# Weight scales, two loads and one block's last spectrum put earlier in a hand-written order of a four-layer S4 and SwiGLU kernel

## The chip, the cores and the metric

The kernel runs on one core of a Trainium2 chip. The metric is the device time of one execution in microseconds (us), the median of several runs. Lines are named by the line numbers of the kernel before (L776 is line 776); the engines are PE (TensorE, matmuls), DVE (VectorE), ACT (ScalarE), POOL (GpSimd) and SP (SyncE, which here only issues DMAs).

## The reference

Four layers work on 2048 tokens of width 512, in float32:

```python
x = A_u
x = x + _A_ref(_layernorm(x), ...)   # S4: K = Re(sum C exp(dt A l) dt B); FFT convolution over the tokens, + u * Dskip
x = x + _B_ref(_layernorm(x), ...)   # SwiGLU: (silu(x @ w_gate) * (x @ w_up)) @ w_down, inner width 1376
x = x + _A_ref(_layernorm(x), ...)   # the same K
x = x + _B_ref(_layernorm(x), ...)   # the same weights
```

The convolution's kernel K has 2048 lags for each of the 512 channels; it and the three FFN matrices are used by both pairs of layers.

## The kernel before, in words

**The work.** The tokens are cut into four blocks of 512. A unit of work is one (layer pair, block): layernorm, convolution, residual, layernorm, FFN, residual. The units run in the order (0,0), (0,1), (0,2), (1,0), (0,3), (1,1), (1,2), (1,3). The convolution is done with discrete Fourier transforms as matmuls: PE makes the spectrum of a block's normalised input (L296 for block 1, tile `pf`), ACT copies it out (L299, tile `u`) and SP stores it (L300, into `udr`); DVE multiplies spectra of inputs and of K (L776 `yk` or `t`, then sums and differences L781 and L782, tile `yf`); PE transforms back (L798, tile `pi`); DVE and ACT put pieces together (L748 to L757, L813 to L828). For each block this is done in eight **steps**, for two halves `h` of the channels and four groups `q` of frequencies, always in the order q = 0, 3, 1, 2. Block b also needs the products with the blocks ahead of it: their spectra are read back from DRAM by SP (L774, tile `uu`; the block's own by L716, tile `u`), and the spectra of K with them (L772, tile `w`).

**Stage one, up to about 257 us**, makes K in chunks of 64 channels. PE's last work in it are the `lags`, many small matmuls (L496, L497) into the PSUM tile `pk`; ACT copies that out (`spread_in`, L507). Its order is a plan, a list of functions with a time each (`at(t, ...)`). The plan also computes norms of the FFN weights (`weights`): squares on ACT (L333), column sums on PE (tile `nrm`, L336) and the largest of them on DVE (`largest`, L339), which empties a list `tops`. From these maxima `scales()` makes one scale for each weight matrix on DVE, in eleven small instructions (L344 to L356).

**The seam, about 257 to 345 us**, does the convolution of block 0, the last spectra of K, and makes f16 weights. Inside `tc.manual_schedule` the order of ACT, DVE, PE and POOL there is the order in which the code is written: `take(it, n)` runs n pieces of a generator. Its parts:

- `take(conv[h], 1)`: one of block 0's eight steps for half h (L776, L781, L782 on DVE, 8 matmuls L798 on PE). The inputs of both halves lie in the same four slots of a tile `mix`; the second half's quarters are loaded over the first's (L713 on SP) as these are used up.
- `first_parts` (PE L580, ACT L581, tile `w0r`) and `later_parts` (`odd`, `rest`: PE L531, ACT L598 or L599, DVE L600, SP store L538): spectra of K, for the block itself and for later blocks.
- `split(hi, lo, load)`: f16 weights in two pieces. ACT makes the high half (L664 for the gate and up matrices, L689 for the down matrix), DVE the low one (L669, L692), and `load` has SP load the next piece (L660, L683, L685), into `wsl` or a staging tile `st`. All three need the scales.
- `norm`: layernorm before the FFN of block 0: statistics on DVE (L203 to L209), ACT's `nn` (L843), PE's transposes (L845, tile `pt`), ACT L848. `direct_size()` (ACT L192, DVE L193) finds a maximum that later scales need.
- `second(*sec[-1])`: block 1's last spectrum (h=1, q=2), two pieces: 8 matmuls L296 from the saved normalised input `n`, then ACT L299 and SP L300.
- `block1`: the steps of block 1's convolution, `ssm(0, 1)`.

Behind the seam (from `product_scale()` on) a scheduler sets the order from priorities. SP's order in the seam is the scheduler's too: it is not one of the four engines of the manual order. Each DMA waits on SP until its tile's buffer is free, and what stands behind it waits as well. The tag `uu` has three buffers in turn: two hold block 1's normalised input for `second`, and the tiles `uu` of block 1's steps take the same ones afterwards.

Of the kernel before, what the change touches and what calls it, by code (L numbers as in the profile page):

```python
# [74 lines left out]
def kernel(ctx, tc, x, a_re, a_im, b_re, b_im, c_re, c_im, log_dt, d_skip,  # L75
# [12 lines left out]
    def tl(shape, name, tag, dt=F32):  # L88
        return sb.tile(shape, dt, name=name, tag=tag, bufs=BUFS[tag])

    def pbig(shape, name):
        return ps.tile(shape, F32, name=name, tag="big", bufs=2)
# [96 lines left out]
    def direct_size():  # L189

        da = tl([1, D], "da", "sg")
        A.activation(da, dsk, AF.Abs)  # L192
        V.tensor_reduce(dmax, da, axis=AX.X, op=OP.max)  # L193


    def stats(src, rows, scale, tag="stats", then=None):

        st = tl([P, 4, 6], "st", tag)
        mv = tl([P, 4, 2], "mv", tag)
        rs = tl([P, 8], "rs", tag)  # L200
        nb = rs[:, 4:]
        for r in range(rows):
            V.bn_stats(st[:, r], src[:, r])  # L203
            V.bn_aggr(mv[:, r], st[:, r])
        V.tensor_scalar(rs[:, :rows], mv[:, :rows, 1], EPS, 1.0 / scale ** 2, OP.add, OP.mult)
        G.tensor_tensor(rs[:, :rows], rs[:, :rows], mhalf[:, :rows], OP.pow)
        if then:
            then()
        V.scalar_tensor_tensor(nb[:, :rows], mv[:, :rows, 0], -1.0, rs[:, :rows], OP.mult, OP.mult)  # L209
        return rs, nb  # L210
# [79 lines left out]
    def direct(b, h, q, n, space=psml):  # L290

        pf = space([P, 2, HD], "pf")
        for i in range(2):
            for c in range(4):
                e = ek[q // 2][:, q % 2, c - 1, i] if c else ef[:, q, i]
                PE.matmul(pf[:, i], lhsT=e, rhs=n[c], start=c == 0, stop=c == 3)  # L296
        yield
        u = tl([P, NQ, 2, DC], "u", "uu")
        A.activation(parted(u), whole(pf), AF.Copy)  # L299
        nc.sync.dma_start(udr[0][b, h, q], u)  # L300
# [3 lines left out]
    def second(h, q, space=psml):  # L304
        if h not in halves:
            halves[h] = n = []
            for cp in range(2):
                t = tl([P, 2, HD], "n1", "uu")
                nc.sync.dma_start(t, ndr[h, cp])
                n += [t[:, 0], t[:, 1]]  # L310
        return direct(1, h, q, halves[h], space)
# [30 lines left out]
    def scales():  # L342
        c2 = sb.tile([P, 3], F32, name="c2")
        V.tensor_reduce(c2, cmx, axis=AX.X, op=OP.max)  # L344
        V.tensor_scalar(c2, c2, 1.01, None, OP.mult)
        ex = sb.tile([P, 3], I32, name="ex")
        V.tensor_scalar(ex, c2.bitcast(I32), 23, None, OP.logical_shift_right)
        V.tensor_scalar(ex, ex, 67, -125, OP.max, OP.add)
        V.tensor_scalar(ex, ex, 1, None, OP.arith_shift_right)
        bits = sb.tile([P, 6], I32, name="bits")  # L350
        V.tensor_scalar(bits[:, 0:3], ex, -1, 141, OP.mult, OP.add)
        V.tensor_scalar(bits[:, 3:4], ex[:, 0:1], 1, 105, OP.mult, OP.add)
        V.tensor_scalar(bits[:, 4:5], ex[:, 0:1], -1, 111, OP.mult, OP.add)
        V.tensor_tensor(bits[:, 5:6], ex[:, 0:1], ex[:, 1:2], OP.add)
        V.scalar_tensor_tensor(bits[:, 5:6], bits[:, 5:6], 107, ex[:, 2:3], OP.add, OP.add)
        V.tensor_scalar(sc6.bitcast(I32), bits, 23, None, OP.logical_shift_left)  # L356
# [143 lines left out]
    def skip(ch, kt, eng):  # L500

        k = kt[0:1, :, 0]
        eng.tensor_tensor(k, k, dsk[:, ch * DC:(ch + 1) * DC].rearrange("p (g d) -> p g d", g=4), OP.add)

    def spread_in(pk):
        ks = tl([P, 4, 16, 16], "ks", "nn")
        A.activation(ks, pk.rearrange("p d (c a) -> p a c d", a=4), AF.Copy)  # L507
        return ks
# [120 lines left out]
    def take(it, n):  # L629
        for _ in range(n):  # L630
            next(it, None)
# [200 lines left out]
    def first_norm(nn2):  # L832


        rows = TB // P
        xt = xs[0][:, :rows]
        nh, nlo = nhl2[:, 0, 0], nhl2[:, 0, 1]
        rs, nb = stats(xt, rows, 256.0, "stats2", then=lambda: split(0, 1))
        yield
        pt = pbig([P, rows, 4, P], "pt")  # L840
        for r in range(rows):
            nn = nn2[:, r]
            A.activation(nn, xt[:, r], AF.Identity, scale=rs[:, r:r + 1], bias=nb[:, r:r + 1])  # L843
            for k in range(4):
                PE.transpose(pt[:, r, k], nn[:, k * P:(k + 1) * P], ident)  # L845
        ptv = pt.rearrange("p r k t -> p k r t")
        nhv = nh.rearrange("p k (r t) -> p k r t", r=rows)
        A.activation(nhv, ptv, AF.Copy)  # L848
        yield
        V.tensor_tensor(nlo.rearrange("p k (r t) -> p k r t", r=rows), ptv, nhv, OP.subtract)  # L850
        yield
# [89 lines left out]
    prods, tops = [], []  # L941
# [11 lines left out]
    with tc.manual_schedule(engines={mybir.EngineType.Activation, mybir.EngineType.DVE, mybir.EngineType.PE, mybir.EngineType.Pool}):  # L953
# [53 lines left out]
        sec = [(h, q) for h in range(2) for q in QORD]  # L1007
        plan = []

        def at(t, f, n=1):  # L1010
            plan.append((t, len(plan), (lambda: take(f, n)) if hasattr(f, "__next__") else f))
# [20 lines left out]
        def factors(c, t):  # L1032

            at(t + 0.2, lambda: upper(ts[c]))

            def tiles(c):
                gs[c] = tl([P, 2, 32, DC], "g", ("ga", "gb")[c % 2])
            if c == 1:
                at(t + 0.1, lambda: tiles(c))
            if c + 1 < NCH:  # L1040
                at(t + 8.05, lambda: tiles(c + 1))
            gg, ge = later(lambda: gen_g(c, ts[c], gs[c])), later(lambda: gen_e(ts[c]))
            for k in range(4):
                at(t + 0.2 + 2 * k, gg, 2)
            at(t + 0.3, ge)
            for k in range(5):
                at(t + 8.2 + k, gg)
            for k in range(4):
                at(t + 22.0 + 0.6 * k, ge, 1 if k < 3 else 100)
# [27 lines left out]
        def weights(n, t0, t1, t2, t3):  # L1077

            us = []

            def product():
                for s, p, m in us:
                    p()
                    if m:
                        tops.append(m)

            def largest():
                while tops:
                    tops.pop(0)()
            at(t0, lambda: us.extend(u for u in (next(nrm, None) for _ in range(n)) if u))  # L1090
            at(t1, lambda: [u[0]() for u in us])
            at(t2, product)
            at(t3, largest)

        starts = [0.0, 31.0, 62.0] + [93.0 + 28.0 * k for k in range(NCH)]
        for i in range(NCH - 1):
            t = starts[i]
            use(i, t)
            factors(i + 1, t)
            second_block(i, t)  # L1100
            if i + 2 < NCH:
                prepare(i + 2, t)
            for k, t0, t1, t2, t3 in ((0, -13.0, 0.25, 13.9, 22.3), (1, 0.3, 14.5, 17.45, 22.9),
                                      (2, 15.0, 26.5, 28.05, 36.0)):
                n = ((3, 3, 0), (3, 3, 0), (3, 3, 0), (3, 2, 0), (3, 2, 0), (3, 3, 0), (3, 3, 3))[i][k]
                if i == NCH - 2 and k == 2:
                    t0, t1, t2, t3 = 15.0, 20.0, 24.0, 27.0
                if n:
                    weights(n, t + t0, t + t1, t + t2, t + t3)
        t = starts[NCH - 1]  # L1110
        late = starts[NCH - 2] + 12.0
        plan.sort()
# [23 lines left out]
        def split(hi, lo, load=0):  # L1136
            for _ in range(load):
                loads.pop(0)()
            for _ in range(hi):
                his.pop(0)()  # L1140
            for _ in range(lo):
                los.pop(0)()
# [13 lines left out]
            yield from itertools.cycle([w[:, j] for w in (wz, wm) for j in range(2)])  # L1156
        slots = slots()

        ks = spread_in(pk)
        odd = later_parts(c - 1, kts[0], (3, 1))  # L1160
        rest = later_parts(c, kts[1])
        bb1 = tl([P, 2, 2, 2, HD], "bb1", "n")
        norm = first_norm(tl([P, 2, D], "nn1", "hf"))
        take(conv[0], 1)
        spread_pe(ks, kts[1])
        skip(c, kts[1], G)
        take(conv[0], 1)
        scales()
        split(1, 0)
        first_parts(c, 0)  # L1170
        take(conv[0], 1)
        split(1, 1)
        split(0, 0, 1)
        first_parts(c - 1, 3)
        split(1, 0)
        take(conv[0], 1)
# [13 lines left out]
        split(0, 0, 1)  # L1190
        take(odd, 2)
        take(conv[1], 1)
        direct_size()
        block1 = ssm(0, 1)
        take(norm, 1)
        take(rest, 2)
        take(odd, 1)
        take(norm, 1)
        take(block1, 1)
        take(rest, 1)  # L1200
        take(odd, 2)
        split(1, 0)
        take(odd, 1)
        take(norm, 1)
# [9 lines left out]
        split(0, 0, 3)  # L1214
        sizes(c, kts[1], ks)
        nn2 = tl([P, 2, D], "nn2", "nn")
        take(second(*sec[-1]), 2)
    pscale = product_scale()
    with tc.high_priority(offset=BOOST // 2):
        while los:  # L1220
# [50 lines left out]
```

## Time and profile before

| what | value |
|---|---|
| runs of the kernel before | median 1156.48 us (1155.17 to 1157.27, 3 runs) |
| the profiled execution's own time | 1156.48 us |
| its span, first to last instruction | 1154.7 us |
| PE busy | 1100.2 us (95%) |
| DVE busy | 998.7 us (86%) |
| ACT busy | 599.1 us (52%) |
| POOL busy | 109.5 us (9%) |

The span is what the views of the trace cover; the 1.8 us around it belong to the execution's own time. Three views are used. The **timeline** lists one engine's instructions: start in us from the span's start, duration in us, engine, line, operation, output<-inputs with shapes, count, and in brackets how long the engine stood idle just before and what ended that idle time. The **waits** add those brackets up by instruction and releaser: us in total, times, longest. The **windows** give for a stretch each engine's busy time with the number of instructions, then the granted PE clock (1 is full speed), the DMA engines' busy share and GB/s. A **DMA issue** row gives the size and the us from the issue's start to the landing of its data.

### The profile page before, as it was taken

To read this page: it belongs to the slowest core of one execution; us is meant where nothing else is said; L and a number is where in the kernel's file an instruction comes from. 1 tells how busy PE (TensorE), PEld (TensorE's weight loads), DVE (VectorE), ACT (ScalarE), POOL (GpSimd) and SP (SyncE) were. 2 spreads that over 40 slices of the span, in tenths; PEclk is the share of its full clock that TensorE was granted. 3 is DMA by queue.
4 is the path that set the end of the run, shared out by engine and by line. 5 is a ranking of instruction groups with operands and counts; after the bars stand their busy time and mean duration, and the time that the engine had idled before them with its cause. 6 is when DMAs were issued, how large, how long until landed. Compare 5 with 4: busy or idle time off the path is not lost.

```text
span 1154.7 us, 24400 instructions
## 1 busy us (share of the span) xinstructions
PE 1100.2 (95%) x9942; PEld 877.6 (76%) x9942; DVE 998.7 (86%) x1585; ACT 599.1 (52%) x1198; POOL 109.5 (9%) x163
## 2 busy tenths in 40 slices
PE   2989999998889999999999999999999999999998
PEld 1878888887776868686868687877778686876875
DVE  8999999988889899999899999989994999973211
ACT  6989889734553453567453534555434352334211
POOL 0112222210000010011010001111000100000000
PEclk9989999999899999999999999999999999999999
DMA  5367777867473446332253454343444145312000
GB/s 209 128 165 165 161 185 170 193 186 244 164 240 110 129 139 207 111 102 74 89 153 124 133 156 150 107 120 105 147 121 140 50 130 160 97 37 48 14 24 19
DMA packets 127314, 150.38 MB, mean 130 GB/s; under 512 B 50897, under 2 KB 75985, under 8 KB 127202
## 3 DMA queue, kind: packets, MB, share of 16 engines
q1 hardware_dynamic: 115298, 123.32, 34.9%
q0 software_dynamic: 11904, 25.50, 9.5%
q8 instruction: 78, 1.28, 0.5%
q14 instruction: 34, 0.28, 0.1%
HBM read 98.70 MB, written 33.82 MB: 115 GB/s over the span
## 4 chain that ended last, share of the span: by engine, by line
PE 35%; DVE 23%; issue 8%; DMA 5%; ACT 3%; SPq 1%; POOL 1%; DVEq 0%; ACTq 0%; POOLq 0%
PE pgu L911 6%; PE pgu L912 6%; PE pgu L914 6%; PE py L926 4%; PE py L927 3%; PE py L928 3%; DVE t L776 3%; DVE yk L779 3%; PE pi L798 2%; PE pf L280 2%; DMA w<-wdr 2%; DVE yk L776 2%; DVE z L228 2%; DVE sg L918 1%; DMA mix<-nn 1%
## 5 line engine op out<-in xcount | busy, mean ns | idle before, releaser
L911 PE MATMUL pgu<-mix,wsl 128*128 128x256 f16 x1280 | 299.0, 273 | 4.3 <-DVE sg L918 3.3
L912 PE MATMUL pgu<-mix,wsl 128*128 128x256 f16 x1280 | 298.6, 273 | 0.0
L914 PE MATMUL pgu<-mix,wsl 128*128 128x256 f16 x1280 | 195.7, 273 | 0.0
L912 PEld LDWEIGHTS <-wsl 128*128 128x128 f16 x1280 | 125.4, 98 | 21.2 <-issue 4.8
L926 PE MATMUL py<-wsl,hh 128*128 128x512 f16 (+1 forms) x352 | 133.4, 379 | 6.1 <-DVE xg L931 4.5
L911 PEld LDWEIGHTS <-wsl 128*128 128x128 f16 x1280 | 125.3, 98 | 16.1
L914 PEld LDWEIGHTS <-wsl 128*128 128x128 f16 x1280 | 125.4, 98 | 14.8
L928 PE MATMUL py<-wsl,hl 128*128 128x512 f16 (+1 forms) x352 | 133.4, 379 | 0.8 <-DVE hl L920 0.8
L776 DVE TENSOR_TENSOR t<-uu,w 128x1024 f32<-128x1024 f32 x96 | 116.9, 1217 | 6.6 <-DMA w<-wdr 6.4
L917 ACT ACTIVATE sg<-pgu,sc 128x512 f32<-128x512 f32 x80 | 54.6, 682 | 130.0 <-PE pgu L914 126.8
L927 PE MATMUL py<-wsl,hh 128*128 128x512 f16 x320 | 121.3, 379 | 0.0
L779 DVE TENSOR_TENSOR yk<-yk,t 128x1024 f32<-128x1024 f32 x96 | 116.8, 1216 | 0.2
L918 DVE SCALAR_TENSOR_TENSOR sg<-pgu,sc,sg 128x512 f32<-128x512 f32 x80 | 59.6, 745 | 52.0 <-ACT sg L917 51.8
L531 PE MATMUL pw<-kt,ek 128*128 128x256 f32 (+1 forms) x384 | 91.8, 376 | 0.0
L919 ACT ACTIVATE hh<-sg 128x512 f16<-128x512 f32 x80 | 50.1, 627 | 76.3 <-DVE sg L918 76.3
L531 PEld LDWEIGHTS pw<-kt,ek 128*128 128x128 f32 x384 | 73.3, 195 | 8.6
L798 PE MATMUL pi<-yl,mix 128*128 128x256 f16 x576 | 78.9, 272 | 0.6 <-DVE yl L228 0.3
L280 PE MATMUL pf<-z,eh 128*128 128x256 f16 x576 | 74.9, 273 | 0.8 <-DVE z L228 0.6
L776 DVE TENSOR_TENSOR yk<-u,w0r 128x1024 f32<-128x1024 f32 x56 | 68.2, 1217 | 0.8 <-ACT u L282 0.8
L920 DVE TENSOR_TENSOR hl<-sg,hh 128x512 f16<-128x512 f32 x80 | 54.8, 685 | 15.5 <-ACT hh L919 15.5
L496 PE MATMUL pk<-re,g 128*32 128x64 f32 x1024 | 65.1, 317 | 2.4 <-DMA g<-g 2.4
L927 PEld LDWEIGHTS <-hh 128*128 128x128 f16 (+1 forms) x352 | 34.5, 98 | 42.7 <-issue 7.3
(238 smaller groups left out, 2164.3 us busy)
## 6 DMA issues: line engine op xcount, KB each, us to landing
uu<-udr SPq DMA_DIRECT2D x96, 256.0 KB, 3.0
w<-wdr SPq DMA_DIRECT2D x96, 256.0 KB, 2.7
udr<-u POOLq DMA_DIRECT2D x32, 256.0 KB, 2.6
g<-g POOLq DMA_DIRECT2D x6, 1024.0 KB, 9.0
udr<-u SPq DMA_DIRECT2D x16, 256.0 KB, 3.5
n<-xdr SPq DMA_DIRECT2D x4, 1024.0 KB, 5.6
kdr<-ks SPq DMA_DIRECT2D x6, 512.0 KB, 2.9
kt<-kdr SPq DMA_DIRECT2D x24, 128.0 KB, 3.1
```

What stands on the lines that cost most here:

```text
L280: PE.matmul(pf[:, o], lhsT=e, rhs=m, start=k == 0, stop=k == len(terms) - 1)
L531: PE.matmul(pw[:, i], lhsT=e, rhs=kt[:, :, c + 4 * k0:4 * k1:4, :].rearrange("p g k d -> p k g d"), start=c == 0, stop=c == 3)
L776: V.tensor_tensor(t, uu.unsqueeze(2).to_broadcast([P, NQ, 2, 2, DC]), w.unsqueeze(3).to_broadcast([P, NQ, 2, 2, DC]), OP.mult)
L779: V.tensor_tensor(yk, yk, t, OP.add)
L798: PE.matmul(pi[:, o], lhsT=e, rhs=m, start=k == 0, stop=k == len(terms) - 1)
L911: PE.matmul(o, lhsT=wgu(wi, k, 0)[:, fs], rhs=nh[:, k], start=k == 0, stop=False)
L912: PE.matmul(o, lhsT=wgu(wi, k, 1)[:, fs], rhs=nh[:, k], start=False, stop=False)
L914: PE.matmul(o, lhsT=wgu(wi, k, 0)[:, fs], rhs=nlo[:, k], start=False, stop=k == 3)
L918: V.scalar_tensor_tensor(sg, pgu[:, 1], sc6[:, 4:5], sg, OP.mult, OP.mult)
L926: PE.matmul(py[:, r], lhsT=hh[:n, f, rc], rhs=wd(f, 0)[:n], start=f == 0, stop=False)
L927: PE.matmul(py[:, r], lhsT=hh[:n, f, rc], rhs=wd(f, 1)[:n], start=False, stop=False)
L928: PE.matmul(py[:, r], lhsT=hl[:n, f, rc], rhs=wd(f, 0)[:n], start=False, stop=f == FT - 1)
```

## The change

Nothing is computed otherwise; instructions stand at other places.

1. The plan's last `weights` group leaves out its `largest`; the code behind the last lags empties `tops` itself, then runs `scales()` and `split(1, 0)` (ACT's first high half, of a gate piece), all ahead of `spread_in` (ACT's copy L507 of the lags). Before, `scales()` and that half stood behind block 0's second step.
2. That piece's low half (`split(0, 1)`) and the load of the next one (`split(0, 0, 1)`) stand ahead of block 0's second step instead of behind its third.
3. `direct_size()` stands behind the first piece of `norm`.
4. The generator of block 1's last spectrum is made ahead of `norm`; its matmuls and two of `odd`'s parts stand ahead of the norm's transposes, its copy and store right behind them. Before, it was the last thing of the seam, and the two parts stood behind block 1's first step.

```diff
--- before.py
+++ after.py
@@ -1090,7 +1090,8 @@
             at(t0, lambda: us.extend(u for u in (next(nrm, None) for _ in range(n)) if u))
             at(t1, lambda: [u[0]() for u in us])
             at(t2, product)
-            at(t3, largest)
+            if t3:
+                at(t3, largest)
 
         starts = [0.0, 31.0, 62.0] + [93.0 + 28.0 * k for k in range(NCH)]
         for i in range(NCH - 1):
@@ -1104,9 +1105,9 @@
                                       (2, 15.0, 26.5, 28.05, 36.0)):
                 n = ((3, 3, 0), (3, 3, 0), (3, 3, 0), (3, 2, 0), (3, 2, 0), (3, 3, 0), (3, 3, 3))[i][k]
                 if i == NCH - 2 and k == 2:
-                    t0, t1, t2, t3 = 15.0, 20.0, 24.0, 27.0
+                    t0, t1, t2, t3 = 15.0, 20.0, 24.0, None
                 if n:
-                    weights(n, t + t0, t + t1, t + t2, t + t3)
+                    weights(n, t + t0, t + t1, t + t2, t3 and t + t3)
         t = starts[NCH - 1]
         late = starts[NCH - 2] + 12.0
         plan.sort()
@@ -1156,21 +1157,25 @@
             yield from itertools.cycle([w[:, j] for w in (wz, wm) for j in range(2)])
         slots = slots()
 
+        while tops:
+            tops.pop(0)()
+        scales()
+        split(1, 0)
         ks = spread_in(pk)
         odd = later_parts(c - 1, kts[0], (3, 1))
         rest = later_parts(c, kts[1])
         bb1 = tl([P, 2, 2, 2, HD], "bb1", "n")
+        last = second(*sec[-1])
         norm = first_norm(tl([P, 2, D], "nn1", "hf"))
         take(conv[0], 1)
         spread_pe(ks, kts[1])
         skip(c, kts[1], G)
+        split(0, 1)
+        split(0, 0, 1)
         take(conv[0], 1)
-        scales()
-        split(1, 0)
         first_parts(c, 0)
         take(conv[0], 1)
-        split(1, 1)
-        split(0, 0, 1)
+        split(1, 0)
         first_parts(c - 1, 3)
         split(1, 0)
         take(conv[0], 1)
@@ -1190,15 +1195,17 @@
         split(0, 0, 1)
         take(odd, 2)
         take(conv[1], 1)
-        direct_size()
         block1 = ssm(0, 1)
         take(norm, 1)
+        direct_size()
         take(rest, 2)
         take(odd, 1)
+        take(last, 1)
+        take(odd, 2)
         take(norm, 1)
+        take(last, 1)
         take(block1, 1)
         take(rest, 1)
-        take(odd, 2)
         split(1, 0)
         take(odd, 1)
         take(norm, 1)
@@ -1214,7 +1221,6 @@
         split(0, 0, 3)
         sizes(c, kts[1], ks)
         nn2 = tl([P, 2, D], "nn2", "nn")
-        take(second(*sec[-1]), 2)
     pscale = product_scale()
     with tc.high_priority(offset=BOOST // 2):
         while los:
```

On DVE, at the end of stage one, the rows of the kernel before read (`cmx` the maxima, `wo` spectra of K, `sc_92` the scales, of whose eleven instructions the first and last are shown, `st_2533` the staged gate piece):

```order
L339 TENSOR_REDUCE cmx<-nrm 128x1
L563 TENSOR_TENSOR wo<-pw,wo 128x2x6x64
L776 TENSOR_TENSOR yk<-mix,w0r 128x1024
...
L776 TENSOR_TENSOR yk<-mix,w0r 128x1024
...
L344 TENSOR_REDUCE c_2718<-cmx 128x3
...
L356 TENSOR_SCALAR sc_92<-bits 128x6
L776 TENSOR_TENSOR yk<-mix,w0r 128x1024
...
L669 SCALAR_TENSOR_TENSOR wsl_2665<-st_2533,sc_92,wsl_2665 128x2x344
L669 SCALAR_TENSOR_TENSOR wsl_2666<-st_2533,sc_92,wsl_2665 128x2x344
```

and those of the changed kernel

```order
L563 TENSOR_TENSOR wo<-pw,wo 128x2x6x64
L339 TENSOR_REDUCE cmx<-nrm 128x1
L344 TENSOR_REDUCE c_2673<-cmx 128x3
...
L356 TENSOR_SCALAR sc_92<-bits 128x6
L776 TENSOR_TENSOR yk<-mix,w0r 128x1024
...
L669 SCALAR_TENSOR_TENSOR wsl_2664<-st_2532,sc_92,wsl_2664 128x2x344
L669 SCALAR_TENSOR_TENSOR wsl_2665<-st_2532,sc_92,wsl_2664 128x2x344
L776 TENSOR_TENSOR yk<-mix,w0r 128x1024
```

The scales moved ahead of block 0's first step, and the two low halves from behind the third step to behind the first. On ACT the high half that they wait for now stands ahead of the copy L507.

On SP, around the same time, the rows of the kernel before read (`mix<-udr` are the reloads of block 0's inputs for the second half, `xg` the residual input, `wsl` and `st` weights):

```order
L713 DMA mix<-udr_114 128x512 x2
L232 DMA xg<-in_A_u_dram 128x4x512
L660 DMA wsl_2668<-in_B_w_up_dram 128x4x344
L660 DMA wsl_2668<-in_B_w_gate_dram 128x4x344
L660 DMA wsl_2668<-in_B_w_up_dram 128x4x344
L232 DMA xg<-in_A_u_dram 128x4x512
L713 DMA mix<-udr_114 128x512
L660 DMA st_2758<-in_B_w_gate_dram 128x4x344
L713 DMA mix<-udr_114 128x512
```

and those of the changed kernel

```order
L713 DMA mix<-udr_114 128x512
L232 DMA xg<-in_A_u_dram 128x4x512
L660 DMA wsl_2667<-in_B_w_up_dram 128x4x344
L660 DMA wsl_2667<-in_B_w_gate_dram 128x4x344
L660 DMA wsl_2667<-in_B_w_up_dram 128x4x344
L660 DMA st_2725<-in_B_w_gate_dram 128x4x344
L232 DMA xg<-in_A_u_dram 128x4x512
L713 DMA mix<-udr_114 128x512 x3
```

The second reload stood ahead of all six large loads and now stands behind them. The staged piece's load moved ahead of the second `xg`.

Further on in SP's rows, where block 1 begins, the kernel before has one load `uu` far earlier, between the staging load and the first of the stores L538 ahead of the reloads, and then here

```order
L685 DMA st_3046<-in_B_w_down_dram 96x512
L538 DMA wdr<-wos 128x3x128
L716 DMA u<-udr_114 128x512
L772 DMA w<-wdr 128x512
L538 DMA wdr<-wos 128x3x128
L716 DMA u<-udr_114 128x512
```

and the changed kernel

```order
L685 DMA st_3058<-in_B_w_down_dram 96x512
L538 DMA wdr<-wos 128x3x128
L716 DMA u<-udr_114 128x512
L774 DMA uu<-udr_114 128x512 x2
L300 DMA udr_114<-u 128x512
L774 DMA uu<-udr_114 128x512 x2
L772 DMA w<-wdr 128x512
```

The first load `uu` of block 1's steps moved here from far ahead, behind a load `u`, and with it come three more loads and the last spectrum's store. On PE, at the transposes, the kernel before has four parts L531 (16 matmuls `pw`) behind block 0's last step, then the transposes `pt`; the changed kernel has

```order
L531 MATMUL pw<-kt_429,ek_83 128x192 x3
L296 MATMUL pf<-n_1626,ef 128x256
L296 MATMUL pf<-n_1626,ek_84 128x256
L296 MATMUL pf<-n_1628,ek_84 128x256 x2
L296 MATMUL pf<-n_1626,ef 128x256
L296 MATMUL pf<-n_1626,ek_84 128x256
L296 MATMUL pf<-n_1628,ek_84 128x256 x2
L531 MATMUL pw<-kt_429,ef 128x192
L531 MATMUL pw<-kt_429,ek_83 128x192 x3
L531 MATMUL pw<-kt_429,ef 128x192
L531 MATMUL pw<-kt_429,ek_83 128x192 x3
L845 MATMUL pt<-ident,nn_2691 128x128 x8
```

Sixteen matmuls, the last spectrum's eight and two parts, moved from behind the transposes to ahead of them.

## The prediction

> **What bounds the kernel now.** I read the totals first, then the windows over the seam and behind it, then the waits, and the timelines last. All sums are made against the profiled execution: 1156.48 us, of which the span is 1154.7 and 1.8 lie around it. It is also the median of the runs shown, so no correction is needed. A measurement of this kernel can tell about 0.2%, 2.3 us, from no change.
>
> The first line is the page's totals. The others are windows: width, busy time (instructions) of PE, its weight loads, DVE, ACT and POOL, then granted clock, DMA share, GB/s.
>
> ```profile
> PE 1100.2 (95%) x9942; PEld 877.6 (76%) x9942; DVE 998.7 (86%) x1585; ACT 599.1 (52%) x1198; POOL 109.5 (9%) x163
> ```
>
> ```profile
> 260.00:270.00 10.00, 10.00 (x79) 8.82 (x68) 6.49 (x10) 6.16 (x7) 0.31 (x1) 1.00 1.06 385
> 290.00:300.00 10.00, 5.21 (x22) 4.92 (x21) 9.83 (x18) 4.18 (x8) 1.34 (x1) 0.66 0.41 142
> 350.00:400.00 50.00, 48.57 (x376) 36.66 (x375) 45.41 (x90) 20.07 (x43) 2.42 (x4) 1.00 0.39 126
> 400.00:450.00 50.00, 48.27 (x405) 36.58 (x403) 49.90 (x80) 26.11 (x49) 6.22 (x7) 1.00 0.49 144
> 350.00:1154.00 804.00, 790.37 (x6585) 607.13 (x6583) 673.55 (x1123) 347.27 (x672) 53.79 (x67) 1.00 0.36 107
> ```
>
> The whole is bound by PE: behind the seam it is busy 790.4 of 804 us. Inside the seam it is not: at 290 to 300 DVE is at 9.8 of 10, and PE falls to 5.2. There DVE sets the pace, and so it does at 400 to 450, where it is at 49.9 of 50. The one place with room on DVE is 350 to 400, 4.6 us. What the change saves on PE counts only as far as DVE lets PE keep it.
>
> The waits of the seam (us in total, times, longest):
>
> ```profile
> ACT ks L507 <- PE pk L497: 7.3, 1, 7.3
> DVE wsl L669 <- ACT wsl L664: 4.8, 1, 4.8
> PE pt L845 <- ACT nn L843: 4.8, 1, 4.8
> DVE t L776 <- DMA w<-wdr: 3.7, 2, 2.6
> PE pgu L911 <- DVE sg L918: 3.3, 1, 3.3
> PE pi L798 <- DVE yf L781: 2.9, 2, 2.7
> DVE wsl L692 <- ACT wsl L689: 2.0, 2, 1.8
> DVE mix L600 <- ACT mix L599: 1.1, 1, 1.1
> ```
>
> The change aims at the second, third and fifth of these.
>
> **Part 1 and 2, scales, first high half and low half.** DVE's and ACT's timelines:
>
> ```profile
> 249.96 0.96 DVE L563 TENSOR_TENSOR wo<-pw,wo 128x768 f32<-128x768 f32 x1 [0.66 <-ACT w0r L559]
> 248.78 0.52 DVE L339 TENSOR_REDUCE cmx<-nrm 128x1 f32<-128x344 f32 x1 [2.08 <-PE nrm L336]
> 250.83 1.22 DVE L776 TENSOR_TENSOR yk<-mix,w0r 128x1024 f32<-128x1024 f32 x1
> 252.88 1.26 DVE L776 TENSOR_TENSOR yk<-mix,w0r 128x1024 f32<-128x1024 f32 x1
> 254.86 0.15 DVE L344 TENSOR_REDUCE c<-cmx 128x3 f32<-128x6 f32 x1
> 256.52 1.23 DVE L776 TENSOR_TENSOR yk<-mix,w0r 128x1024 f32<-128x1024 f32 x1
> 263.34 1.78 DVE L669 SCALAR_TENSOR_TENSOR wsl<-st,sc,wsl 128x688 f16<-128x688 f32 x2 [4.79 <-ACT wsl L664]
> 265.04 1.22 DVE L776 TENSOR_TENSOR yk<-mix,w0r 128x1024 f32<-128x1024 f32 x1
> 268.36 1.22 DVE L776 TENSOR_TENSOR yk<-mix,w0r 128x1024 f32<-128x1024 f32 x1
> 270.46 1.23 DVE L776 TENSOR_TENSOR yk<-mix,w0r 128x1024 f32<-128x1024 f32 x1
> ```
>
> ```profile
> 264.58 0.28 ACT L581 ACTIVATE w0r<-pw 128x128 f32<-128x128 f32 x1 [1.27 <-PE pw L580]
> 268.19 0.37 ACT L581 ACTIVATE w0r<-pw 128x256 f32<-128x256 f32 x1
> ```
>
> The eleven scale instructions take 1.66 us (254.86 to 256.52) wherever they stand. With L563 done at 250.9 and the maximum 0.52 behind it, the scales are ready at about 253.0 instead of 256.5. ACT then makes the first high half in the 7.3 us in which it waited for the lags, and the DVE wait of 4.79 goes. From 253.0 a step costs 2.05 (250.83 to 252.88) and the low half 1.7 to 1.8: the fourth step starts at 253.0 + 3 × 2.05 + 1.78 = 260.9. The fourth to the fifth took 3.32, so the fifth could start at 264.3; but its `w0r` comes from ACT at 264.86, behind a PE that is busy 10.00 of 10.00 there. It starts at 264.9 instead of 268.36. The sixth's `w0r` comes at 268.56, so by these rows alone it starts at 268.6 instead of 270.46: **-1.9 us**. More of the 4.79 isn't to be had, since PE is late next.
>
> **What the moved loads cost.** The sixth step reads the second reload L713, which now stands on SP behind both `xg` and four weight loads. SP's timeline, and the DMA issues of three stretches: the second `xg`, the reload issued right behind it, and the two reloads ahead of all large loads (size, us from issue to landing):
>
> ```profile
> 257.18 0.38 SPq L232 DMA_DIRECT2D xg<-in_A_u_dram  x1
> 259.60 1.73 SPq L232 DMA_DIRECT2D xg<-in_A_u_dram  x1
> ```
>
> ```profile
> xg<-in_A_u_dram SPq DMA_DIRECT2D x1, 1024.0 KB, 11.4
> mix<-udr SPq DMA_DIRECT2D x1, 256.0 KB, 10.3
> ...
> mix<-udr SPq DMA_DIRECT2D x2, 256.0 KB, 3.1
> ```
>
> The loads cannot start before 257.2, when the lags free their buffers. The second `xg` was issued at 259.60 and landed 11.4 later, 271.0. By the window's 385 GB/s, one of 688 KB takes 1.85 us and one of 256 KB takes 0.7. With the staged piece now ahead of `xg` and the reload behind, the reload lands at 271.0 + 1.85 + 0.7 = 273.5. The sixth step then starts 3.1 later than before, not 1.9 earlier: **+3.1 us** on DVE. The bounds are -1.9 (the reload overtakes) and +3.1. I take +3.1, since the reload issued behind the large loads needed 10.3 us for the same 256 KB that took 3.1 ahead of them.
>
> The Trainium skill, "DMA: Bandwidth & Descriptors", section "Queues, rings and completion order", says that each DMA engine consumes a ring in order but that completion is not FIFO per issuing engine. If the second half let the reload finish first, the term would be -1.9. The 11.4 us row of the second `xg`, which fits a queue emptied in order, speaks against it here.
>
> PE's gap ahead of the seventh transform, 2.7 us in the waits, grows by the same lateness to about 5.2.
>
> **Part 3, `direct_size`.** Its DVE maximum leaves the chain ahead of the norm's last factor L209: **-0.6 us**.
>
> ```profile
> 290.19 0.67 DVE L193 TENSOR_REDUCE dmax<-da 1x1 f32<-1x512 f32 x1
> 294.28 0.15 DVE L209 SCALAR_TENSOR_TENSOR rs<-mv,rs 128x2 f32<-128x2 f32 x1
> 294.81 1.21 DVE L776 TENSOR_TENSOR yk<-u,w0r 128x1024 f32<-128x1024 f32 x1
> 295.95 1.22 DVE L776 TENSOR_TENSOR t<-uu,w 128x1024 f32<-128x1024 f32 x1
> ```
>
> L209 then stands at 294.28 + 3.1 - 0.6 = 296.8.
>
> **Part 4, the last spectrum.** On PE it fills the wait for the norm. Windows of PE alone (width, PE busy, clock, DMA share, GB/s):
>
> ```profile
> 279.60:283.20 3.60, 3.60 (x8) 0.54 0.12 12
> 295.30:299.70 4.40, 4.37 (x17) 0.50 0.87 294
> 328.00:330.60 2.60, 2.54 (x13) 0.50 0.80 109
> ```
>
> The idle 4.79 and the half clock behind it (4.4 us at 0.50, so 2.2 lost) go: -7.0 on PE. The wait of 3.3 ahead of `pgu` and its half clock (2.6 at 0.50, 1.3 lost) should go too, since ACT no longer makes so many high halves ahead of the first activation of the FFN: -4.6. Against these stand +2.5 ahead of the seventh transform and, since DVE is late, a new wait at the third `pgu` for the second L918, about 3.5 and 1.7 of half clock. PE's own sum is -7.0 - 4.6 + 2.5 + 5.2 = **-3.9 us**.
>
> The Trainium skill, "TensorE: Matmul & The Clock Gate", section "What's actually happening", has the clock halve after an idle window of about 3.4 us. Here 2.73 us idle were enough (0.54 at 279.6 to 283.2). By the page the gap ahead of the seventh transform would start to cost clock only now, 1.8 us more; by the rows it costs that already, and I count none.
>
> On DVE the same move costs a wait. Block 1's first load `uu` had a free buffer and was issued long ahead, before the reloads; now the last spectrum's tiles hold it longer, and on SP it stands behind the load `u`, which waits until DVE has done `yk`.
>
> ```profile
> 296.06 0.34 SPq L716 DMA_DIRECT2D u<-udr  x1
> ```
>
> ```profile
> uu<-udr SPq DMA_DIRECT2D x96, 256.0 KB, 3.0
> ```
>
> L716 was issued at the end of `yk` (294.81 + 1.21). Now `yk` ends near 298.6, `uu` is issued by 299.5 and lands 3.0 later, at 302.5; DVE, in order, could have used it at 298.5. That is **+4.1 us**. The bounds are 0, if other DVE work moved ahead covers it, and 4.7, with slower landings as near the large loads; I take the row's median.
>
> **The sum.** DVE: +3.1 - 0.6 + 4.1 = 6.6. The waits of 1.1 (L600) and 1.8 (L692) go, because DVE now comes later than ACT: 3.7. Of the 3.7 us for `w` in block 1's next steps I count half as gone, 1.9, because SP issues some of those loads earlier and some later: 1.8. A wait for the FFN's activation L917 takes their place, 1.2: **+3.0 us** at the end of the seam. PE is 3.9 ahead by its own sum, but its transforms for block 1 wait for DVE, and DVE is then full to 450 but for the 4.6 us at 350 to 400. I count none of these as absorbed, since DVE waits there for products of PE and ACT that come as late. Forecast: 1156.5 + 3.0 = **1159.5**, its own range 1157.8 to 1162.
>
> **The rivals.**
>
> 1. *The reload isn't held* (it overtakes, or lands with the small loads). Then the term +3.1 is -1.9: 3.0 - 5.0 = -2.0, with a little of the first wait following, about 1154. For it speaks that the loads run on 16 engines; against it the landing rows. The page of the Trainium skill named above, "DMA: Bandwidth & Descriptors", would allow it; no row here shows it. Chance 0.15.
> 2. *PE sets the end.* DVE's lag is taken up by its 4.6 us at 350 to 400, and PE keeps its -3.9: 1152.6. For it speaks PE's 98% behind the seam; against it DVE's 49.9 of 50. Chance 0.15.
> 3. *The uu wait is short.* Where the last spectrum's store and loads go early, the +4.1 is about 1: 3.0 - 3.1 = -0.1, 1156.4. Chance 0.16.
> 4. *Nothing is given back.* Stalls add: +3.1 - 0.6 + 4.7 + 1.2 = 8.4, less the 1.1 and 1.8 that must go, is 5.5, with one more half-clock stretch of up to 1.7: 1162 to 1164. For it speaks that each PE wait was followed by half clock. Chance 0.17.
>
> Rivals 1 and 2 end on the other side: rival 2 decides when DVE's idle at 350 to 400 falls by more than 3 us.
>
> **How the numbers follow.** The forecast has 0.37; some three quarters of it (0.27) lie over 1158.8, so slower is 0.27 + 0.17 = 0.44, same 0.10 + 0.16 = 0.26, faster 0.15 + 0.15 = 0.30. The range 1152.5 to 1164 reaches from rival 2 to rival 4.
>
> **What would show it.** Right: no wait at the first L669; the sixth step waits for `mix` and starts near 273.5; PE idle of 5 us ahead of the seventh transform, none ahead of `pt`; DVE waits some 4 us for `uu` near 300. Wrong: the sixth step at 268.6; `uu` landed before DVE asks; DVE's idle at 350 to 400 near 1.5.

## The result, and the profile after

The changed kernel takes 1160.6 us (median) against 1156.03 for the kernel before in the same series: 1.0037 times as long, interval 1.0026 to 1.0048. It is slower by 4.6 us where 3.0 were forecast. One of its six executions took 1620.7 us at a granted clock of 0.66 and is left out of the ratio; the other five lie between 1159.1 and 1161.5. Its profiled execution took 1160.61 us with a span of 1158.8, so 1.8 us lie around the span as before, and the two profiles differ by 4.1.

The waits of PE and DVE in the seam of the changed kernel, the larger rows (us in total, times, longest):

```profile
DVE yk L776 <- DMA mix<-udr: 7.8, 1, 7.8
PE pi L798 <- DVE yf L781: 6.8, 2, 5.3
...
DVE t L776 <- DMA udr<-u: 5.5, 1, 5.5
PE pgu L911 <- DVE sg L918: 5.4, 1, 5.4
...
PE pw L531 <- DVE wos L600: 1.7, 1, 1.7
DVE wsl L692 <- ACT wsl L689: 1.4, 1, 1.4
DVE sg L918 <- ACT sg L917: 1.2, 1, 1.2
```

The waits that the change aimed at are gone: no row for L669 behind ACT's L664, none for the transposes `pt`. Two DVE waits on transfers stand in their place, 7.8 and 5.5 us. DVE's timeline at the two places, and at the norm's last factor (L209) between them:

```profile
264.54 1.22 DVE L776 TENSOR_TENSOR yk<-mix,w0r 128x1024 f32<-128x1024 f32 x1 [0.56 <-ACT w0r L581]
274.41 1.23 DVE L776 TENSOR_TENSOR yk<-mix,w0r 128x1024 f32<-128x1024 f32 x1 [7.84 <-DMA mix<-udr]
...
297.66 0.15 DVE L209 SCALAR_TENSOR_TENSOR rs<-mv,rs 128x2 f32<-128x2 f32 x1
297.73 0.67 DVE L193 TENSOR_REDUCE dmax<-da 1x1 f32<-1x512 f32 x1
...
298.79 1.20 DVE L776 TENSOR_TENSOR yk<-u,w0r 128x1024 f32<-128x1024 f32 x1
305.51 1.23 DVE L776 TENSOR_TENSOR t<-uu,w 128x1024 f32<-128x1024 f32 x1 [5.52 <-DMA udr<-u]
```

The fifth step is 3.8 us earlier than before (268.36), the sixth 4.0 us later (270.46). SP's timeline shows why:

```profile
253.65 0.33 SPq L713 DMA_DIRECT2D mix<-udr  x1
...
261.18 1.83 SPq L232 DMA_DIRECT2D xg<-in_A_u_dram  x1
263.11 2.64 SPq L713 DMA_DIRECT2D mix<-udr  x3
...
300.46 0.92 SPq L774 DMA_DIRECT2D uu<-udr  x2
```

The DMA issue rows of the second reload and of the first `uu` alone:

```profile
mix<-udr SPq DMA_DIRECT2D x1, 256.0 KB, 11.2
...
uu<-udr SPq DMA_DIRECT2D x1, 256.0 KB, 5.0
```

The first reload was issued at 253.65 and is there in time; the second is issued at 263.11, behind everything, and its 256 KB take 11.2 us to land. The wait at 305.51 is put down to a store, `udr<-u`; but the first `uu`, issued at 300.46, has 5.0 us to its landing, which puts that at about 305.4, right ahead of DVE's start. So this wait is read as one for `uu`; in e1, e5, e11 and e12 below the same wait is put down to `uu<-udr` itself.

The windows of the seam and of the stretch behind it, as shown of before:

```profile
260.00:270.00 10.00, 10.00 (x75) 8.95 (x67) 5.59 (x9) 4.83 (x6) 0.36 (x1) 1.00 1.06 383
...
290.00:300.00 10.00, 10.00 (x58) 9.59 (x57) 9.72 (x20) 2.11 (x5) 1.36 (x1) 1.00 0.31 92
...
350.00:400.00 50.00, 48.77 (x361) 36.37 (x360) 44.97 (x85) 17.68 (x40) 3.05 (x3) 0.98 0.41 125
```

At 290 to 300 PE is full where it was at 5.2. That gain is spent elsewhere: DVE stands idle for 7.8 us up to 274.4 and for 5.5 up to 305.5, and PE idles 5.3 us ahead of the seventh transform and 5.4 ahead of the third `pgu`, each followed by a low clock (two rows of PE's timeline, then windows of PE alone: width, PE busy, clock, DMA share, GB/s):

```profile
276.22 1.99 PE L798 MATMUL pi<-yf,mix 128*128 128x256 f32 x8 [1.48 <-DVE yf L781]
283.54 5.88 PE L798 MATMUL pi<-yf,mix 128*128 128x256 f32 x16 [5.33 <-DVE yf L781]
```

```profile
283.50:289.40 5.90, 5.86 (x17) 0.65 0.44 127
...
336.10:338.70 2.60, 2.57 (x13) 0.50 0.09 35
```

How the lag travels is read best at one instruction that recurs, L931 (the end of an FFN block, 32 times). The first, the eleventh and the last of them, of the kernel before:

```profile
366.03 0.75 DVE L931 SCALAR_TENSOR_TENSOR xg<-py,sc,xg 128x512 f32<-128x512 f32 x1
...
647.64 0.73 DVE L931 SCALAR_TENSOR_TENSOR xf<-py,sc,xf 128x512 f32<-128x512 f32 x1
...
1150.51 0.75 DVE L931 SCALAR_TENSOR_TENSOR xg<-py,sc,xg 128x512 f32<-128x512 f32 x1 [7.38 <-PE py L928]
```

and of the changed kernel:

```profile
371.32 0.74 DVE L931 SCALAR_TENSOR_TENSOR xg<-py,sc,xg 128x512 f32<-128x512 f32 x1
...
651.73 0.75 DVE L931 SCALAR_TENSOR_TENSOR xf<-py,sc,xf 128x512 f32<-128x512 f32 x1
...
1154.58 0.75 DVE L931 SCALAR_TENSOR_TENSOR xg<-py,sc,xg 128x512 f32<-128x512 f32 x1 [7.38 <-PE py L928]
```

The lag is 5.3 at the first, 4.1 at the eleventh, and 4.1 at the last. Behind the seam 1.2 us of it, less than a quarter, are taken up.

### The profile page after: what moved, and what is told of

Same layout as the page of the kernel before. It is cut to its first block, busy times and chain, and to the rows that moved or that the text cites. A ratio compares the mean times of both kernels' runs of the same rounds, so it can differ in the third digit from the quotient of the medians.

```text
span 1158.8 us, 24411 instructions
## 1 busy us (share of the span) xinstructions
PE 1098.8 (95%) x9942; PEld 876.1 (76%) x9942; DVE 998.8 (86%) x1585; ACT 598.4 (52%) x1198; POOL 111.6 (10%) x163
## 4 chain that ended last, share of the span: by engine, by line
DVE 39%; PE 35%; issue 11%; DMA 9%; ACT 4%; POOL 1%; SPq 1%; DVEq 0%; ACTq 0%; POOLq 0%
DVE t L776 5%; DVE yk L779 5%; PE pgu L911 4%; PE pgu L912 4%; PE pgu L914 4%; PE pw L531 4%; DVE yk L776 3%; PE py L926 3%; PE py L927 3%; DVE z L228 3%; PE py L928 3%; PE pi L798 3%; DMA g<-g 2%; DVE sg L918 2%; DVE hl L920 2%
## 5 line engine op out<-in xcount | busy, mean ns | idle before, releaser
L917 ACT ACTIVATE sg<-pgu,sc 128x512 f32<-128x512 f32 x80 | 54.5, 682 | 120.9 <-PE pgu L914 118.3
L531 PE MATMUL pw<-kt,ek 128*128 128x256 f32 (+1 forms) x384 | 91.5, 375 | 0.0
L531 PEld LDWEIGHTS pw<-kt,ek 128*128 128x128 f32 x384 | 72.9, 194 | 8.8
```

The source lines that it names most:

```text
L531: PE.matmul(pw[:, i], lhsT=e, rhs=kt[:, :, c + 4 * k0:4 * k1:4, :].rearrange("p g k d -> p k g d"), start=c == 0, stop=c == 3)
```

## The experiments

Theory A is the prediction's: two DVE waits on transfers make the lag, and it is carried to the end. Theory B, rival 2: PE sets the end, and what DVE gains or loses in the seam is absorbed. Theory C: the order that the scheduler makes behind the seam costs the time. After the first four runs it became theory D: that order moves the end by some us in any version, whatever the seam does. To tell D from A, DVE's instructions behind the seam were compared one by one between the programs, tile numbers left out; "match" below is the share that stands in matching order with the kernel before. The landmark "first L931" comes from one profile of each kernel, and it wanders: e8, with every instruction of DVE and ACT in the order of the kernel before and a median within 0.1 us of it, stands 0.7 us ahead of it at the first L931 and 2.4 at the eleventh. So differences of one or two us between landmarks say little by themselves.

| run | median us | ratio to before, interval | first L931 (before 366.0) | match |
|---|---|---|---|---|
| changed kernel | 1160.6 | 1.0037 (1.0026 to 1.0048) | 371.3 | 0.89 |
| e1 all reloads on POOL | 1157.7 | 1.0018 (1.0007 to 1.0028) | 367.2 | 0.87 |
| e2 last spectrum's own buffer | 1164.4 | 1.0083 (1.0066 to 1.0099) | 368.0 | 0.62 |
| e3 e1 and e2 | 1153.0 | 0.9977 (0.9966 to 0.9989) | 366.1 | 0.96 |
| e4 parts 1, 2 only | 1159.4 | 1.0031 (1.0020 to 1.0042) | 368.9 | 1.00 |
| e5 parts 3, 4 only | 1159.2 | 1.0031 (1.0019 to 1.0043) | 370.1 | 0.87 |
| e6 e5, own buffer | 1163.4 | 1.0071 (1.0059 to 1.0084) | 368.7 | 0.59 |
| e7 own buffer, reloads 2 to 4 on POOL | 1159.6 | 1.0034 (1.0021 to 1.0047) | 361.2 | 0.62 |
| e8 before, all reloads on POOL | 1155.3 | 0.9999 (0.9990 to 1.0008) | 365.3 | 1.00 |
| e9 e4, reload 2 on POOL | 1153.6 | 0.9984 (0.9975 to 0.9993) | 362.7 | 1.00 |
| e10 own buffer, reload 2 on POOL | 1151.5 | 0.9965 (0.9955 to 0.9976) | 361.5 | 0.97 |
| e11 changed, reloads 2 to 4 on POOL | 1154.8 | 0.9987 (0.9974 to 0.9999) | 363.3 | 0.89 |
| e12 e11, one load u on POOL | 1155.1 | 0.9990 (0.9980 to 1.0000) | 362.3 | 0.89 |

**e1**, all four reloads through POOL's queue:

```diff
-                                nc.sync.dma_start(u4[:, qn], udr[0][0, 1, qn])
+                                nc.gpsimd.dma_start(u4[:, qn], udr[0][0, 1, qn])
```

> The changed kernel with the reloads L713 issued by POOL's queue instead of SP's, so that they no longer stand behind the weight loads. Theory A (the two DMA waits on DVE are the cost and are carried to the end): the 7.8 us wait of the sixth step falls below 1, the norm's L209 moves from 297.7 to 292.5 or so, the uu wait stays at 4 to 6, and the time falls by 3 to 5 us, to 1156 to 1157.5. Theory B (PE sets the end and the lag is absorbed behind the seam): the waits move as in A, but the time stays within 1 us of 1160.6. Theory C (the new order behind the seam costs the time, weights and third pgu late): the time stays above 1159.

Measured 1157.7. The reload wait fell to 4.4 us only, since POOL issues even the first reload at 261.83, and it is now the fifth step that waits. L209 came at 293.3, near A's 292.5, and the `uu` wait stayed at 5.5. 2.9 us of the time went, less than the 4.1 at the first L931, and the time is 0.2 above A's range; B, within 1 us of 1160.6, and C, above 1159, both miss.

**e2**, the last spectrum's copy in a buffer of the tag `sg`, so that all three `uu` buffers are as before:

```diff
-        u = tl([P, NQ, 2, DC], "u", "uu")
+        u = tl([P, NQ, 2, DC], "u", tag)
...
-        last = second(*sec[-1])
+        last = second(*sec[-1], tag="sg")
```

> The changed kernel with the last spectrum's copy in a buffer of another tag (sg), so that block 1's first uu load has a free buffer again. Theory A: uu is loaded before the reloads, DVE's wait of 5.5 us ahead of its first use goes, the reload wait of 7.8 stays; time 3 to 5 us less, 1156 to 1157.5. Theory B: waits as in A, time within 1 us of 1160.6. Theory C: time above 1159.

Measured 1164.4, a miss for A and B; of the three only C, with its bound of 1159, holds. The `uu` wait is gone, with two waits for `w`, 4.0 us together, in its place; the first L931 is 3.3 us earlier than in the changed kernel, yet the end is 3.8 us later. The loss arises far behind the seam: at the eleventh L931 (652.6) the lag against before is 5.0, at the nineteenth 7.4. This raised theory D.

**e3**, both edits:

```diff
+                                nc.gpsimd.dma_start(u4[:, qn], udr[0][0, 1, qn])
...
+        last = second(*sec[-1], tag="sg")
```

> Both edits together. Theory A: both waits gone, what is left is the gain that the change aimed at: the sixth step near 268.6, no wait at the transposes, no uu wait; 1150 to 1154, faster than the kernel before. Theory B: within 1.5 us of the kernel changed as it is, or at most down to 1158. Theory C: 1157 to 1160, not faster than the kernel before.

Measured 1153.0, faster than the kernel before, as A has it and C does not. The sixth step came at 270.3, not 268.6, since POOL issues the first reload late here too (a wait of 4.4 for it); the first L931 is only level with before. Its profiled execution, 1157.48, was the longest of its runs, so the landmark says less than the median here.

**e4**, parts 1 and 2 of the change alone:

```diff
+        while tops:
+            tops.pop(0)()
+        scales()
+        split(1, 0)
         ks = spread_in(pk)
...
         skip(c, kts[1], G)
+        split(0, 1)
+        split(0, 0, 1)
         take(conv[0], 1)
-        scales()
-        split(1, 0)
...
```

> The kernel before with parts 1 and 2 of the change alone (scales, first high and low halves). Theory A: the reload wait of about 7.8 us appears, the sixth step is 3 to 4 us later than in the kernel before, the transposes keep their PE wait; time 2 to 4 us over the kernel before, 1158 to 1160. Theory B: 1156 to 1157. Theory C (the last spectrum's move remakes the order): 1155 to 1157.

Measured 1159.4, 3.6 us over the kernel before. DVE's order behind the seam is that of before in every instruction, so a new order there is not what costs it.

**e5**, parts 3 and 4 alone, and **e6**, the same with the own buffer (the added lines only):

```diff
+        last = second(*sec[-1])            # e6: second(*sec[-1], tag="sg")
...
         take(norm, 1)
+        direct_size()
         take(rest, 2)
         take(odd, 1)
+        take(last, 1)
+        take(odd, 2)
         take(norm, 1)
+        take(last, 1)
```

> The kernel before with parts 3 and 4 of the change alone (last spectrum and two parts ahead of the transposes, direct_size behind). Theory A: no reload wait and the sixth step at 270.5 as in the kernel before, no PE wait at the transposes, but a DVE wait of 4 to 6 us for uu; the lag at DVE's first L931 is 0 to 3 us; time 1155 to 1159. Theory D (in every version the order made behind the seam moves the end by some us whatever the seam does): the lag between the first and the last L931 changes by more than 2 us.

> As e5, with the last spectrum's copy in a buffer of its own tag. Theory A: no uu wait, the lag at DVE's first L931 is -5 to -1 us; by this alone 1151 to 1155. Theory D: the end differs from that by more than 2 us, as in e2, and the difference arises behind the seam.

e5: 1159.2, by the mechanism of A with a `uu` wait of 5.8, but just over its upper end, with a lag of 4.0 at the first L931 where 0 to 3 were expected. Theory D as first put, for any version, fails here: between the first and the last L931 the lag changes by 1.6 us, not by more than 2. e6: the wait is gone, the first L931 is 1.3 us earlier than in e5, though not earlier than in the kernel before as A expected; and the end is 4.2 us later than e5's. A's 1151 to 1155 is missed, and A says nothing of a loss behind the seam; D does.

**e7**, the changed kernel with own buffer and the first reload left on SP.

```diff
+                                (nc.gpsimd if i or qn else nc.sync).dma_start(u4[:, qn], udr[0][0, 1, qn])
```

> The changed kernel with only the second and later reloads on POOL's queue (the first stays on SP, ahead of the loads) and the last spectrum in its own buffer. Theory A: the fifth step is at 264.5 again instead of 268 in e3, the sixth at 268.6 to 269, no uu wait; the seam ends 1 to 3 us earlier than in e3: 1150 to 1153. Theory D: anything from 1150 to 1160, with the seam's landmarks as in A.

Measured 1159.6, where A had 1150 to 1153: the seam is as A says, 4.8 us ahead of the kernel before at the first L931, but the median is 4.2 us behind it.

**e8**, the control: the kernel before with e1's line, all reloads on POOL:

```diff
+                                nc.gpsimd.dma_start(u4[:, qn], udr[0][0, 1, qn])
```

> The kernel before with all reloads on POOL's queue. The kernel before does not wait for a reload, so theory A expects the fifth and sixth step within 1 us of 268.4 and 270.5 and the time within 1.5 us of the kernel before. Theory D: up to 5 us off, arising behind the seam.

1155.3, no difference. Where no step waits for a reload, the queue changes nothing in the time.

**e9**, e4 with one DMA moved, the second reload. PE's, DVE's and ACT's orders are the same as e4's in every instruction.

```diff
+                                (nc.gpsimd if qn == QORD[1] else nc.sync).dma_start(u4[:, qn], udr[0][0, 1, qn])
```

> As e4 (parts 1 and 2 alone), with one DMA moved: the second reload L713 goes through POOL's queue. The order on PE, DVE and ACT is that of e4, and DVE's order behind the seam that of the kernel before. Theory A: the 7.5 us wait of the sixth step falls below 2.5, the step starts 5 us earlier, near 269; at the first L931 DVE is 3 to 6 us earlier than in e4, and as the order behind the seam is fixed, 3 to 5 us of it reach the end: 1154 to 1156.5. Theory B (absorbed behind the seam): within 1 us of e4, 1158.4 to 1160.4.

Measured 1153.6, 5.8 us less than e4. The sixth step in e4 and then in e9:

```profile
274.32 1.22 DVE L776 TENSOR_TENSOR yk<-mix,w0r 128x1024 f32<-128x1024 f32 x1 [7.53 <-DMA mix<-udr]
```

```profile
268.23 1.22 DVE L776 TENSOR_TENSOR yk<-mix,w0r 128x1024 f32<-128x1024 f32 x1 [1.98 <-DMA mix<-udr]
```

It starts 6.1 us earlier and the end comes 5.8 earlier, 0.4 below the range that A gave. With the order held fixed, the lag of this wait is carried nearly in full: A, and not B.

**e10**, the changed kernel with the own buffer and only the second reload on POOL:

```diff
+        last = second(*sec[-1], tag="sg")
...
+                                (nc.gpsimd if qn == QORD[1] else nc.sync).dma_start(u4[:, qn], udr[0][0, 1, qn])
```

> As e7 (all parts, last spectrum in its own buffer), but only the second reload through POOL; the third and fourth stay on SP. The seam's instructions stand as in e7, but the order that comes out behind the seam is nearly that of the kernel before (97 of 100 DVE instructions in matching order, 62 in e7). Theory A with D: first L931 within 1.5 us of e7's 361.2, and the lead of about 4.8 us over the kernel before is carried: 1150 to 1152.5. If the seam's lead were worth nothing at the end (theory B): 1155 to 1157. If e7's loss were due to the seam itself and not to the order behind it: 1158 to 1161.

Measured 1151.5, the fastest of all. PE up to 342 us and DVE up to 350 have e7's instructions in e7's order, and of the reloads only the third and fourth stand on another queue; the order behind the seam is another. The first L931 and the seventeenth, of e7 and then of e10, and of the kernel before the seventeenth:

```profile
361.23 0.74 DVE L931 SCALAR_TENSOR_TENSOR xg<-py,sc,xg 128x512 f32<-128x512 f32 x1
...
810.97 0.74 DVE L931 SCALAR_TENSOR_TENSOR xg<-py,sc,xg 128x512 f32<-128x512 f32 x1
```

```profile
361.46 0.75 DVE L931 SCALAR_TENSOR_TENSOR xg<-py,sc,xg 128x512 f32<-128x512 f32 x1
...
802.08 0.74 DVE L931 SCALAR_TENSOR_TENSOR xg<-py,sc,xg 128x512 f32<-128x512 f32 x1
```

```profile
809.04 0.74 DVE L931 SCALAR_TENSOR_TENSOR xg<-py,sc,xg 128x512 f32<-128x512 f32 x1
```

From 0.2 us apart, e7 falls 8.9 us behind e10. The window 550 to 850 of e7, of e10 and of the kernel before shows a part of it as lost work, 3.9 us of PE and 8.0 of DVE:

```profile
550.00:850.00 300.00, 294.10 (x2490) 230.74 (x2489) 285.25 (x466) 141.04 (x269) 21.11 (x28) 0.99 0.41 126
```

```profile
550.00:850.00 300.00, 297.98 (x2525) 233.66 (x2523) 293.30 (x480) 142.77 (x274) 24.91 (x29) 1.00 0.43 129
```

```profile
550.00:850.00 300.00, 297.24 (x2540) 235.09 (x2538) 291.19 (x480) 143.70 (x275) 24.61 (x28) 1.00 0.43 128
```

PE is busy for 294.1 us in e2 and e7 and 293.9 in e6, the three versions with a match of 0.6, and for 297.1 to 298.0 in the eleven others, the kernel before among them. The own buffer alone is not the cause, since e3 and e10 have it too and lose nothing; nor is the queue of the later reloads, since e11 has that and loses nothing. So theory D holds for these three, as far as the comparison goes; which swap in the order costs the time was not tried.

**e11**, the changed kernel with the reloads as in e7, and DVE's and ACT's orders as in the changed kernel throughout:

```diff
+                                (nc.gpsimd if i or qn else nc.sync).dma_start(u4[:, qn], udr[0][0, 1, qn])
```

> The changed kernel with the second and later reloads on POOL's queue, the first on SP; nothing else. DVE's and ACT's order is that of the changed kernel throughout, so this holds the order behind the seam fixed. Theory A: the reload wait falls from 7.8 to about 2, the uu wait stays at 5 to 6, the first L931 is 4 to 6 us earlier than in the changed kernel (371.3), and 4 to 6 us of it reach the end: 1154.5 to 1156.5. Theory B (absorbed behind the seam): 1159 to 1161.

Measured 1154.8, 5.8 us less than the changed kernel. The first L931 is 8.0 us earlier, more than expected; some 2 of it are lost on the way. A holds.

**e12**, e11 with the load `u` of block 1's third step on POOL:

```diff
-                            nc.sync.dma_start(u, udr[0][b, h, q])
+                            (nc.gpsimd if (b, h, q) == (1, 0, 1) else nc.sync).dma_start(u, udr[0][b, h, q])
```

> As e11, with one more DMA moved: the load u of block 1's third step goes through POOL, so that the first uu load no longer stands behind a load that waits for DVE's yk. DVE's and ACT's order unchanged. Theory A: uu is issued 1 to 2 us earlier and lands 1.5 to 2.5 us earlier, DVE's wait for it falls from about 5.5 to 3 to 4, and the time by 1 to 2.5 us from e11's. If that load is not what holds uu (it still waits for its buffer and for the weight load ahead of it), the wait and the time stay within 0.7 us of e11's.

Measured 1155.1, the same as e11. SP's issue of `uu` and DVE's wait for it, in e11 and then in e12:

```profile
294.70 0.89 SPq L774 DMA_DIRECT2D uu<-udr  x2
```

```profile
299.13 1.23 DVE L776 TENSOR_TENSOR t<-uu,w 128x1024 f32<-128x1024 f32 x1 [4.90 <-DMA uu<-udr]
```

```profile
293.39 0.96 SPq L774 DMA_DIRECT2D uu<-udr  x2
```

```profile
299.02 1.23 DVE L776 TENSOR_TENSOR t<-uu,w 128x1024 f32<-128x1024 f32 x1 [4.99 <-DMA uu<-udr]
```

The load is issued 1.3 us earlier and lands at the same time. So it isn't the place behind `u` that makes the wait.

## Why the prediction was right, point by point

- **Scales, high and low halves.** Right. The scales are ready at 252.4 (forecast 253.0), the L669 wait is gone, the fifth step starts at 264.54 (264.9), held by `w0r`.
- **The second reload.** Right in mechanism and nearly in size. The sixth step starts at 274.41, forecast 273.5: +4.0 against before, not +3.1. With the reload on POOL's queue it starts at 268.2 in e9, where it still waits 2.0 for the reload, and at 268.6 in e11, where it waits for `w0r`, as the forecast's other bound has it. The term's whole worth, forecast 5.0, is 5.8 in the time of e4 against e9 and again 5.8 in the changed kernel against e11, which moves the third and fourth reload too. Rival 1 is out.
- **`direct_size`.** L209 came at 297.66, forecast 296.8; the 0.9 is the sixth step's. The 0.6 is there: from the sixth step to L209 it is 23.81 us in e4, with the maximum ahead, and 23.25 in the changed kernel. But it should not have stood in DVE's sum. L193 now comes right behind L209 and still ahead of `yk`, so that `yk` starts at 298.79, the whole 4.0 us later than before (294.81), and nothing of the 0.6 reaches block 1.
- **PE.** The gap ahead of `pt` went, and the gap at the third `pgu` is 5.39 (3.5). The one ahead of the seventh transform is 5.33 (5.2), but that match is luck: 2.7 and the forecast's lateness of 3.1 give 5.8, and the real lateness of 4.0 went into two gaps, this one and one of 1.48 ahead of the sixth transform, which was not forecast. A wait of 1.7 at L531 for DVE was not foreseen.
- **The uu load.** The wait is 5.5, not 4.1, and over the upper bound of 4.7. The step that failed is "lands 3.0 later": `uu` was issued 0.5 behind the end of `yk`, sooner than the forecast's 0.9, but took 5.0 to land. Of the two stated causes, the buffer holds: with a buffer of its own for the last spectrum the wait is gone (e2, e3, e6, e7, e10). The place behind `u` fell with e12. In all runs with this wait two weight loads of 704 KB together are issued ahead of it, the first by 1.6 to 2.7 us, on the same queue; that they hold it up fits, but wasn't tried alone. In e10 the first `uu` is issued at 290.51, 1.3 ahead of these two, and lands in 2.7, while one issued at 294.56, 2.7 behind the first of them, takes 6.5. How much of the time the `uu` wait costs isn't shown by itself either: every version that keeps part 4 and is without the wait has another order behind the seam.
- **What is given back.** The `w` waits of 3.7 went in full, not by half, and come back (2.6 to 6.9) in the five versions with the own buffer, where no `uu` wait covers them; the L600 wait of 1.1 went; L692 kept 1.4 of its 2.0, where 1.8 were to go; the L917 wait came at 1.2 as forecast.
- **The sum.** +3.0 was forecast at the seam's end and for the time. It is +5.3 at the first L931, +4.1 from the eleventh on, and +4.6 in the medians. By the rows: `yk` 4.0 later, + 5.5 for `uu`, - 1.1 for L600, - 0.6 for L692, - 3.7 for `w`, + 1.2 for L917 is +5.3. (Behind the seam, up to the first L931, DVE waits 1.0 us more for `w` and has three instructions fewer, about 1.0 us, so these two cancel.) Against the forecast that is 0.9 more for the reload, 0.6 for `direct_size`, 1.4 for `uu` and 1.2 for L692, and 1.8 less for `w`. So the sum came near because errors both ways made up for each other in part, and because 1.2 us were taken up behind the seam, which the forecast had at nothing.
- **Nothing absorbed at 350 to 400.** Right there: DVE idles 5.0 us, 4.6 before, and e9 against e4 shows the carry. Of the lag 1.2 us went by the eleventh L931. Rival 2 is out.
- **What was missing.** No rival named the order that the scheduler makes anew behind the seam. In the changed kernel itself it cost little: e11 has the same order on DVE and ACT and ends 1.1 us below the kernel before, from a first L931 that is 2.7 ahead. But it was worth 8 us between e7 and e10, more than any term of the sum.

So both halves of the change do in the seam what was meant, and each brought a late transfer: alone they cost 3.6 us (e4) and 3.9 (e5), together 4.6, so they don't add up. The first half with its reload mended gains 1.9 (e9); the second alone with its `uu` mended was tried only with another order behind the seam (e6). With the two transfers mended and the old order nearly kept (e10) the change is worth 4.0 us the other way.

## What to carry to other kernels

When code is moved in a written order, list the DMAs whose order is not written with it: here one reload of 256 KB fell behind 4.8 MB of loads that were needed later, and cost 5.8 us. Here PE and DVE were both busy for about 97% of the time or more from 550 to 850, and of a wait taken away most came through to the end (5.8 us where the step started 6.1 earlier in e9, 5.8 of the 8.0 at the first L931 in e11). So a wait is priced by its length rather than by its engine's share of the time, less the waits behind it that it covers: the `uu` wait of 5.5 hid 3.7 of waits for `w`. And where a scheduler orders the rest, compare its order between the versions before reading a time: a version may lose in that order what it won by the edit.

## What the runs showed of the hardware

A load issued on POOL's queue got past those waiting on SP's. In e9 the reload on POOL was issued at 261.93, between the second `xg` (260.63) and the other reloads (262.64) on SP:

```profile
mix<-udr SPq DMA_DIRECT2D x2, 256.0 KB, 11.4
mix<-udr POOLq DMA_DIRECT2D x1, 256.0 KB, 6.2
```

It landed in 6.2 us, and those two reloads took 11.4 (the median); the second `xg`, 12.2 us in e4, took 13.5. The Trainium skill, "DMA: Bandwidth & Descriptors", section "Queues, rings and completion order", says that a DMA engine goes round the queues that have work for it, a packet at a time; the 6.2 against 11.4 agree with it.

PE's clock fell to 0.65 over the 5.9 us behind the 5.3 us gap and to 0.50 over the 2.6 behind the 5.4 us gap, while the transform behind a gap of 1.48 us (276.22) took 1.99 us, as one behind a gap of 0.17 did in the kernel before (1.97, at 283.38).
